# Attention and FFN interleaved on one core: score bursts of three chunks, PV one head at a time, FFN blocks partly in a score bank

## The chip, the cores and the metric

One NeuronCore of one Trainium2 chip. The metric is the device time of one execution in microseconds (us). The fast executions of the kernel before agree within about 1%. "Fast" and "slow" below are the states that each run lists; comparisons use fast runs. A ratio is the mean time of one kernel's fast runs over that of the other's of the same rounds, on the same chip, so it is not quite the ratio of the medians that are quoted.

Engines in the profile: PE is the matmul engine (TensorE), PEld its weight load, ACT is ScalarE (the exponentials), DVE is VectorE (copies, multiplies), POOL issues the loads, SPq is the queue of the transposing DMAs.

## The reference

```python
# q, k, v: (8, 8, 1152, 64); x: (4608, 512); dff = 1024
q_pool = q.reshape(B, H, S // 2, 2, D).mean(axis=3)      # 576 query rows a head
scores = matmul(q_pool, k.T) / sqrt(D)                   # softmax over 1152 keys
attn_out = softmax(scores) @ v                           # -> x, (B*576, 512)
a = x @ w1;  b = x @ w2
out = ((a * b) @ w3) @ w_out                             # T = w3 @ w_out is formed once
```

## The kernel before

Heads are worked in 32 pairs. A pair has 9 blocks of 128 keys times 576 queries; this stream of columns is cut in 324 chunks of 512. One chunk is a score tile of two PSUM banks (one a head), one exponential of 128x1024, and nine or so PV matmuls (exponentials times V) for both heads together, each with a 128x128 block of exponentials as weights. A burst is the score matmuls of the chunks of one iteration. FFN units of 512 tokens (96 matmuls of 512 columns, worked in blocks, each the matmuls into one bank) fill PE between them, as soon as their tokens are there. PE executes its matmuls in the order of the program.

The kernel uses eight PSUM banks: two score tiles (4), one accumulator for both heads (2), two FFN banks (2).

```python
def scores(c):                                   # one chunk, both heads (64-row tiles of PE)
    t = psum.tile([128, 2, CH], FP32, tag="psc", bufs=2, name="psc")
    ...
def attend(J, i):                                # PV: both heads, one after the other
    ...
        po[P] = psum.tile([128, 2, 512], FP32, tag="po", bufs=1, name="po")
    for u in range(2):
        nc.tensor.matmul(po[P][:, u, VW * i:VW * i + D + 1], er[:, u, r:r + 128],
                         vts[P % 4][:, u, j, 0:D + 1], ...)
def normalize(P):                                # DVE, once a pair: reciprocal, multiply
    ...
def bank(pre, wide):                             # FFN blocks: a bank of their own
    if not wide:
        return psum.tile([128, 512], FP32, tag="ff", bufs=2, name=pre)
...
for it in range(NIT):                            # 162 iterations of two chunks
    scores(2 * it);     expo(2 * it)
    scores(2 * it + 1); expo(2 * it + 1)
    ...
    for J, i in ready: attend(J, i)              # about 18 PV matmuls
    if last: normalize(...)
    fill(due)                                    # about five FFN matmuls
```

The softmax here doesn't subtract the row's maximum and nothing guards it: scores larger than these inputs give would overflow.

Of the kernel before, what the change touches and what calls it, by code (L numbers as in the profile page):

```python
# [18 lines left out]
RING = 4608  # L19
# [4 lines left out]
def kernel(  # L24
# [21 lines left out]
    T_AT = (8, 14)  # L46

    T_MM, T_TR, T_SC, T_AV = 0.216, 0.06, 0.63, 0.061
    PACE0, PACE1 = 2.2, 2.19
# [13 lines left out]
    w3T = const.tile([128, NF, NF, 128], FP16)  # L63
    wosb = const.tile([128, NF, dm], FP16)
# [86 lines left out]
    def prep_pe(P):  # L151
# [3 lines left out]
        t2 = psum.tile([128, 1024], FP16, tag="ff", bufs=2, name="t2")  # L155
        t1 = psum.tile([128, 1024], FP16, tag="ff", bufs=2, name="t1")
# [17 lines left out]
    def scores(c):  # L174
        t = psum.tile([128, 2, CH], FP32, tag="psc", bufs=2, name="psc")
# [20 lines left out]
    po = {}  # L196

    def attend(J, i):

        P, j = divmod(J, NJ)  # L200
        if j == 0 and i == 0:
            po[P] = psum.tile([128, 2, 512], FP32, tag="po", bufs=1, name="po")
        f = 128 * i if i < 4 else SQ - 128
        r = (J * SQ) % RING + f
        for u in range(2):
            nc.tensor.matmul(  # L206
                po[P][:, u, VW * i:VW * i + D + 1],
                er[:, u, r:r + 128],
                vts[P % 4][:, u, j, 0:D + 1],
                start=(j == 0 and i == 0), stop=(j == NJ - 1 and i == 4),  # L210
                skip_group_check=True)

    def normalize(P):
        acc = po.pop(P)[:, :, 0:5 * VW].rearrange("p u (i w) -> p u i w", w=VW)
        rz = ab.tile([128, 2, 5, 1], FP32, tag="rz", bufs=2, name="rz")
        nc.vector.reciprocal(out=rz, in_=acc[:, :, :, D:D + 1])  # L216
        xn = ab.tile([128, 5, 2, D], FP16, tag="xn", bufs=3, name="xn")
        nc.vector.tensor_tensor(  # L218
            out=xn.rearrange("p i u d -> p u i d"), in0=acc[:, :, :, 0:D],
            in1=rz.to_broadcast([128, 2, 5, D]), op=ALU.mult)  # L220
# [21 lines left out]
    def bank(pre, wide):  # L242
        if not wide:
            return psum.tile([128, 512], FP32, tag="ff", bufs=2, name=pre)
        return psum.tile([128, 2, 512], FP32, tag="psc", bufs=2, name=pre)[:, 0, :]

    def w3_transpose(c):
        t = psum.tile([128, 1024], FP16, tag="ff", bufs=2, name="w3t")
        for a in range(NF):
            nc.tensor.transpose(t[:, 128 * a:128 * a + 128],  # L250
                                w3h[c // 4][:, c % 4, 128 * a:128 * a + 128], ident)
        nc.vector.tensor_copy(out=w3T[:, c].rearrange("p a f -> p (a f)"), in_=t)

    def gen_T(half):

        cs = range(4 * half, 4 * half + 4)
        w3_transpose(cs[0])
        yield 8 * T_TR, True
        for c in cs:
            if c + 1 in cs:  # L260
                w3_transpose(c + 1)
                yield 8 * T_TR, True
            pt = bank("pT", False)
            for a in range(NF):
                nc.tensor.matmul(pt, w3T[:, c, a, :], wosb[:, a, :],  # L265
                                 start=(a == 0), stop=(a == NF - 1))
                if a < NF - 1:
                    yield T_MM, False
            nc.vector.tensor_copy(out=T16[:, c, :], in_=pt)  # L269
            yield T_MM, True  # L270

    def gen_ffn(t, tail):
        t0 = 512 * t
        gT = ffp.tile([128, NF, 512], FP16, tag="g", name="gT")
        for ft in range(NF):
            pa = bank("pa", tail and ft % 2)
            for mc in range(NC):
                nc.tensor.matmul(pa, w1sb[:, mc, ft * 128:ft * 128 + 128],  # L278
                                 xT[:, mc, t0:t0 + 512],
                                 start=(mc == 0), stop=(mc == NC - 1))  # L280
                if mc < NC - 1:
                    yield T_MM, False
            asb = ffp.tile([128, 512], FP32, tag="asb", name="asb")
            if tail:
                nc.scalar.copy(out=asb, in_=pa)  # L285
            else:
                nc.vector.tensor_copy(out=asb, in_=pa)  # L287
            yield T_MM, True
            pb = bank("pb", tail and ft % 2)
            for mc in range(NC):  # L290
                nc.tensor.matmul(pb, w2sb[:, mc, ft * 128:ft * 128 + 128],  # L291
                                 xT[:, mc, t0:t0 + 512],
                                 start=(mc == 0), stop=(mc == NC - 1))
                if mc < NC - 1:
                    yield T_MM, False
            nc.vector.tensor_mul(out=gT[:, ft, :], in0=pb, in1=asb)  # L296
            yield T_MM, True
        for i in range(4):
            pp = bank("pp", tail and i % 2)
            for ft in range(NF):  # L300
                nc.tensor.matmul(pp, gT[:, ft, 128 * i:128 * i + 128], T16[:, ft, :],  # L301
                                 start=(ft == 0), stop=(ft == NF - 1))
                if ft < NF - 1:
                    yield T_MM, False
# [54 lines left out]
    for it in range(NIT):  # L359
# [40 lines left out]
        if last:  # L400
            ready = ready[:last[0] + 1]
# [47 lines left out]
```

## Time and profile before

| | before |
|---|---|
| time | 449.42 us median of the first 3 runs (448.94 to 453.55) |
| PE / ACT / DVE busy | 93% / 73% / 44% |
| chain that ended last | 83% PE |
| one iteration (two chunks) in the middle | 2.26 us on average (most 2.0 to 2.5), 1.13 us a chunk |
| exponentials back to back | 0.92 us a chunk |

From the page of the kernel before: busy time of the engines, and the first line of the chain that ended last.

```profile
PE 419.4 (93%) x5168; PEld 223.1 (50%) x5168; DVE 198.2 (44%) x347; ACT 329.8 (73%) x350; POOL 70.0 (16%) x107
PE 83%; DMA 5%; ACT 4%; DVE 4%; issue 3%; SPq 1%; POOL 0%; ACTq 0%; DVEq 0%; POOLq 0%
```

PE bounds it. What PE waited for stands in the waits of engine PE: who waited for whom, then us in total, times, longest.

```profile
PE t_126 L158 <- DVE qp L119: 6.1, 1, 6.1
PE psc L187 <- DMA qT<-qp: 5.3, 1, 5.3
PE psc L187 <- ACT er L193: 4.2, 10, 0.7
PE po L206 <- DVE xn L218: 0.2, 1, 0.2
```

The 6.1 us are the start. The 5.3 us are one stall at 110 us. Waits of PV for the accumulator (`po`) are 0.2 us, and FFN lines do not wait for ACT at all.

One iteration in the timeline of the kernel before (start us, duration us, engine, line, output<-input, count; idle time before it in brackets):

```profile
231.44 0.61 PE L187 MATMUL psc<-qT,kT 64*128 64x512 f16 x6
231.93 1.94 ACT L193 ACTIVATE er<-psc 128x1024 f16<-128x1024 f32 x2 [0.49 <-PE psc L187]
231.98 0.72 PE L206 MATMUL po<-vt_78,er 128*128 128x65 f16 x18
232.54 1.02 PE L291 MATMUL pb<-xT,w2sb 128*128 128x512 f16 x4
233.40 0.38 PE L278 MATMUL pa<-xT,w1sb 128*128 128x512 f16 x1
233.71 0.39 PE L187 MATMUL psc<-qT,kT 64*128 64x128 f16 x4
```

Read PE by starts, because durations of matmuls overlap (a 512-column matmul is listed with 0.38 us and the next starts 0.215 us later). The burst takes 0.54 us, 18 PV 0.56, four FFN matmuls 0.86; the single `pa` takes 0.31 to the next score, 0.1 more than to another FFN matmul. ACT starts 0.49 us after the burst's first matmul.

The start-to-start times agree with the Trainium skill ("TensorE: Matmul & The Clock Gate", Back-to-back issue gap), which gives N/2.4 + 2.5 ns for a warm PE: it says 216 ns for 512 columns, and the trace has 215; worked out for 65 columns it gives an estimate of 29.6, and the trace has 29 to 30.

### The profile page before, as it was taken

The numbers are of one execution on the slowest core, as the hardware profiler recorded it, in microseconds if no ns is written. First come the engines' busy times: TensorE is split into PE (matmuls) and PEld (weight loads), VectorE is DVE, ScalarE is ACT, GpSimd is POOL, SyncE is SP. The second block draws the span as 40 slices with busy tenths as digits, with TensorE's granted clock in tenths as the row PEclk, the third lists the DMA queues.
The fourth block names the chain that finished last, engine by engine and source line by source line (L and its number), as shares of the span: only waits on it lengthen the run. The fifth ranks groups of instructions, "written<-read, shape, count | busy, mean of one in ns | idle before, by whom it ended". The sixth has DMA issues, their size and how long they took to land.

```text
span 448.8 us, 12036 instructions
## 1 busy us (share of the span) xinstructions
PE 419.4 (93%) x5168; PEld 223.1 (50%) x5168; DVE 198.2 (44%) x347; ACT 329.8 (73%) x350; POOL 70.0 (16%) x107
## 2 busy tenths in 40 slices
PE   2889898998699999999999999999999999989995
PEld 1555454554355555555555555545555555544442
DVE  2255454565235544554345444544554444433130
ACT  2977776777388888888888888888888888823332
POOL 7312130113011111111111111111100000000000
PEclk9999999999699999999999999999999999999999
DMA  8999999659999899999999999969882460131304
GB/s 137 209 188 206 208 190 182 94 94 126 154 182 150 129 111 204 167 144 126 148 179 130 134 173 183 132 117 164 167 155 57 92 106 18 15 70 39 89 6 93
DMA packets 94468, 59.11 MB, mean 132 GB/s; under 512 B 66256, under 2 KB 83664, under 8 KB 94416
## 3 DMA queue, kind: packets, MB, share of 16 engines
q0 software_dynamic: 25168, 33.56, 48.5%
q1 hardware_dynamic: 69248, 24.79, 35.1%
q8 instruction: 40, 0.66, 0.6%
q14 instruction: 12, 0.10, 0.1%
HBM read 67.11 MB, written 9.44 MB: 171 GB/s over the span
## 4 chain that ended last, share of the span: by engine, by line
PE 83%; DMA 5%; ACT 4%; DVE 4%; issue 3%; SPq 1%; POOL 0%; ACTq 0%; DVEq 0%; POOLq 0%
PE po L206 20%; PE psc L187 20%; PE pb L291 13%; PE pa L278 13%; PE pp L301 12%; ACT er L193 4%; PE pT L265 3%; DMA qT<-qp 3%; DMA vst<-in_v_dram 1%; DVE xn L218 1%; DVE kT L168 1%; PE w3t L250 1%; DMA out_dram<-osb 1%; DVE T_73 L269 0%; DVE osb L310 0%
## 5 line engine op out<-in xcount | busy, mean ns | idle before, releaser
L193 ACT ACTIVATE er<-psc 128x1024 f16<-128x1024 f32 x324 | 313.4, 1022 | 72.6 <-PE psc L187 69.8
L187 PE MATMUL psc<-qT,kT 64*128 64x512 f16 (+7 forms) x1152 | 109.2, 290 | 11.8 <-DMA qT<-qp 5.3
L206 PEld LDWEIGHTS <-er 128*128 128x128 f16 x2880 | 97.5, 98 | 35.5 <-issue 32.0
L187 PEld LDWEIGHTS <-kT 64*128 64x128 f16 x1152 | 44.4, 95 | 96.0 <-issue 84.5
L291 PE MATMUL pb<-xT,w2sb 128*128 128x512 f16 x288 | 79.7, 379 | 2.4 <-DVE osb L310 1.3
L278 PE MATMUL pa<-xT,w1sb 128*128 128x512 f16 x288 | 79.1, 379 | 1.2 <-DVE asb L287 0.7
L296 DVE TENSOR_TENSOR gT<-pb,asb 128x512 f16<-128x512 f32 x72 | 49.6, 688 | 64.1 <-PE pb L291 63.6
L301 PE MATMUL pp<-T_73,gT 128*128 128x512 f16 x288 | 71.4, 384 | 0.0
L287 DVE COPY asb<-pa 128x512 f32<-128x512 f32 x56 | 38.5, 688 | 47.1 <-PE pa L278 47.1
L90 POOL DMA_DIRECT2D kst<-in_k_dram x32 | 23.0, 718 | 221.3 <-DVE kc L135 175.1
L310 DVE TENSOR_SCALAR osb<-pp 128x512 f32<-128x512 f32 x28 | 19.3, 690 | 53.8 <-PE pp L301 51.4
L301 PEld LDWEIGHTS <-gT 128*128 128x128 f16 x288 | 25.7, 99 | 24.7 <-issue 1.1
L278 PEld LDWEIGHTS <-w1sb 128*128 128x128 f16 x288 | 25.8, 97 | 23.8 <-issue 0.7
L291 PEld LDWEIGHTS <-w2sb 128*128 128x128 f16 x288 | 25.4, 97 | 23.6 <-issue 1.6
L206 PE MATMUL po<-vt_80,er 128*128 128x65 f16 x720 | 29.6, 196 | 0.3 <-DVE xn L218 0.2
L206 PE MATMUL po<-vt_77,er 128*128 128x65 f16 x720 | 29.7, 195 | 0.0
L206 PE MATMUL po<-vt_78,er 128*128 128x65 f16 x720 | 28.7, 193 | 0.0
L206 PE MATMUL po<-vt_79,er 128*128 128x65 f16 x720 | 28.7, 193 | 0.0
L285 ACT COPY asb<-pa 128x512 f32<-128x512 f32 x16 | 9.4, 585 | 24.5 <-PE pa L278 24.5
L218 DVE TENSOR_TENSOR xn<-po,rz 128x640 f16<-128x640 f32 x32 | 26.4, 824 | 1.3 <-DVE rz L216 0.2
L97 POOL DMA_DIRECT2D vst<-in_v_dram x32 | 23.4, 732 | 16.6 <-DMA w3h<-in_moe_w_dram 10.3
L216 DVE RECIPROCAL rz<-po 128x10 f32<-128x10 f32 x32 | 7.1, 220 | 38.3 <-PE po L206 38.2
(80 smaller groups left out, 147.8 us busy)
## 6 DMA issues: line engine op xcount, KB each, us to landing
qst<-in_q_dram POOLq DMA_DIRECT2D x32, 288.0 KB, 7.1
kst<-in_k_dram POOLq DMA_DIRECT2D x32, 288.0 KB, 5.2
vst<-in_v_dram POOLq DMA_DIRECT2D x32, 288.0 KB, 9.0
out_dram<-osb SPq DMA_DIRECT2D x72, 128.0 KB, 3.3
w3h<-in_moe_w_dram POOLq DMA_DIRECT2D x2, 1024.0 KB, 20.5
wosb<-in_moe_w_out_dram POOLq DMA_DIRECT2D x1, 1024.0 KB, 19.5
xT<-xn SPq DMA_TRANSPOSE x64, 3.6
w1sb<-in_moe_w_dram POOLq DMA_DIRECT2D x1, 1024.0 KB, 22.0
```

The costliest lines, as they stand in the source:

```text
L90: nc.gpsimd.dma_start(out=kst[P].rearrange("p u j d -> p u (j d)"), in_=k[b, h0:h0 + 2].rearrange("u (p j) d -> p u (j d)", j=NJ))
L97: nc.gpsimd.dma_start(out=vst[P].rearrange("p u j d -> p u (j d)"), in_=v[b, h0:h0 + 2].rearrange("u (p j) d -> p u (j d)", j=NJ))
L187: nc.tensor.matmul(t[:, u, o:o + ln], kT[P][s, j, :], qv[s, f0:f0 + ln], start=True, stop=True)
L193: nc.scalar.activation(out=er[:, :, r:r + CH], in_=psc.pop(c), func=AF.Exp, bias=0.0, scale=SCALE)
L206: nc.tensor.matmul(po[P][:, u, VW * i:VW * i + D + 1], er[:, u, r:r + 128], vts[P % 4][:, u, j, 0:D + 1], start=(j == 0 and i == 0), stop= ...
L218: nc.vector.tensor_tensor(out=xn.rearrange("p i u d -> p u i d"), in0=acc[:, :, :, 0:D], in1=rz.to_broadcast([128, 2, 5, D]), op=ALU.mult)
L278: nc.tensor.matmul(pa, w1sb[:, mc, ft * 128:ft * 128 + 128], xT[:, mc, t0:t0 + 512], start=(mc == 0), stop=(mc == NC - 1))
L287: nc.vector.tensor_copy(out=asb, in_=pa)
L291: nc.tensor.matmul(pb, w2sb[:, mc, ft * 128:ft * 128 + 128], xT[:, mc, t0:t0 + 512], start=(mc == 0), stop=(mc == NC - 1))
L296: nc.vector.tensor_mul(out=gT[:, ft, :], in0=pb, in1=asb)
L301: nc.tensor.matmul(pp, gT[:, ft, 128 * i:128 * i + 128], T16[:, ft, :], start=(ft == 0), stop=(ft == NF - 1))
L310: nc.vector.tensor_scalar_mul(out=osb, in0=pp, scalar1=1.0 / (SCL * SCL))
```

## The change

The intent: fewer, longer score bursts, so that PE changes less often between score matmuls (half the rows a head) and the others, and a third score tile so that bursts do not wait for exponentials. The banks for it (6) come from two places: PV works one head at a time, so the accumulator is one bank, and FFN has only one bank of its own; every other FFN block goes into a score tile "in turn". The core of the diff:

```diff
-RING = 4608
+RING = 9216                                     # PV now runs about eight chunks behind
+    BURST = 3
-        t = psum.tile([128, 2, CH], FP32, tag="psc", bufs=2, name="psc")
+        t = psum.tile([128, 2, CH], FP32, tag="psc", bufs=3, name="psc")
...
-            po[P] = psum.tile([128, 2, 512], FP32, tag="po", bufs=1, name="po")
+            po[P, u] = psum.tile([128, 512], FP32, tag="po", bufs=1, name="po")
...                                              # normalize(P, u): once a head
+        if kind == "F":
+            return psum.tile([128, w], dt, tag="ff", bufs=1, name=pre)
+        return psum.tile([128, 2, w], dt, tag="psc", bufs=3, name=pre)[:, 0, :]
...                                              # x @ w1: kind X; x @ w2: kind F
+        for w in range(BURST):
+            scores(BURST * it + w)
+            expo(BURST * it + w)
...
-        lead = 0.5 if prepped < NPE else min(1.6, 0.5 + 0.5 * (prepped - NPE + 1))
+        if prepped < NP and at >= prepped - (0.65 if prepped < NPE else 1.75):
...
+        if peek() == "F":                       # a block left from the iteration before
+            run()
...                                              # parts: PV up to a change of heads, and after
+        head = 12 if len(parts[0]) > 12 else len(parts[0])
+        pv(parts[0][:head])
+        if x_free and peek() == "X" and done < quota:
+            run()
+        pv(parts[0][head:])
+        if peek() == "F" and done < quota:
+            run(quota)
+        pv(parts[1])
```

The output rows of the seven units inside the loop are made in halves of 256 columns. T = w3 @ w_out is formed at once and not in two halves. The count of score, PV and FFN columns stays the same. K and Q of the first eight pairs are still transposed by PE, now into a score tile; those of the later pairs are transposed by DMA, and their lead (how many pairs ahead they are prepared) is now 1.75 from the first such pair on.

More of the change, by code (lines that the diff above doesn't have):

```diff
@@ L45 @@
     NPE = 8
-    T_AT = (8, 14)
-    T_MM, T_TR, T_SC, T_AV = 0.216, 0.06, 0.63, 0.061
-    PACE0, PACE1 = 2.2, 2.19
+    BURST = 3
     SCALE = 0.5 * float(D) ** -0.5
@@ L62 @@
     T16 = const.tile([128, NF, dm], FP16)
-    w3T = const.tile([128, NF, NF, 128], FP16)
-    wosb = const.tile([128, NF, dm], FP16)
+    wosb = xT[:, :, NT - 1024:NT].rearrange("p m (h f) -> p m h f", h=2)
     er = const.tile([128, 2, RING], FP16)
@@ L154, in prep_pe @@
         kc = kcs.pop(P)
-        t2 = psum.tile([128, 1024], FP16, tag="ff", bufs=2, name="t2")
-        t1 = psum.tile([128, 1024], FP16, tag="ff", bufs=2, name="t1")
+        t12 = psum.tile([128, 2, 1024], FP16, tag="psc", bufs=3, name="t12")
+        t1, t2 = t12[:, 0, :], t12[:, 1, :]
         for c in range(NJ):
@@ L194, in expo, with attend, ready, normalize @@
                              bias=0.0, scale=SCALE)
-    po = {}
-    def attend(J, i):
-        P, j = divmod(J, NJ)
-        if j == 0 and i == 0:
-            po[P] = psum.tile([128, 2, 512], FP32, tag="po", bufs=1, name="po")
-        f = 128 * i if i < 4 else SQ - 128
-        r = (J * SQ) % RING + f
-        for u in range(2):
-            nc.tensor.matmul(
-                po[P][:, u, VW * i:VW * i + D + 1],
-                er[:, u, r:r + 128],
-                vts[P % 4][:, u, j, 0:D + 1],
-                start=(j == 0 and i == 0), stop=(j == NJ - 1 and i == 4),
-                skip_group_check=True)
-    def normalize(P):
-        acc = po.pop(P)[:, :, 0:5 * VW].rearrange("p u (i w) -> p u i w", w=VW)
-        rz = ab.tile([128, 2, 5, 1], FP32, tag="rz", bufs=2, name="rz")
-        nc.vector.reciprocal(out=rz, in_=acc[:, :, :, D:D + 1])
-        xn = ab.tile([128, 5, 2, D], FP16, tag="xn", bufs=3, name="xn")
-        nc.vector.tensor_tensor(
-            out=xn.rearrange("p i u d -> p u i d"), in0=acc[:, :, :, 0:D],
-            in1=rz.to_broadcast([128, 2, 5, D]), op=ALU.mult)
+    po, xns = {}, {}
+    def attend(n):
+        P, m = divmod(n, 90)
+        u, m = divmod(m, 45)
+        j, i = divmod(m, 5)
+        if m == 0:
+            po[P, u] = psum.tile([128, 512], FP32, tag="po", bufs=1, name="po")
+        f = 128 * i if i < 4 else SQ - 128
+        r = ((P * NJ + j) * SQ) % RING + f
+        nc.tensor.matmul(
+            po[P, u][:, VW * i:VW * i + D + 1], er[:, u, r:r + 128],
+            vts[P % 4][:, u, j, 0:D + 1],
+            start=(m == 0), stop=(m == 44), skip_group_check=True)
+    def ready(n, chunks):
+        P, m = divmod(n, 90)
+        j, i = divmod(m % 45, 5)
+        return (P * NJ + j) * SQ + min(128 * i + 128, SQ) <= chunks * CH
+    def normalize(P, u):
+        acc = po.pop((P, u))[:, 0:5 * VW].rearrange("p (i w) -> p i w", w=VW)
+        rz = ab.tile([128, 5, 1], FP32, tag="rz", bufs=2, name="rz")
+        nc.vector.reciprocal(out=rz, in_=acc[:, :, D:D + 1])
+        if u == 0:
+            xns[P] = ab.tile([128, 5, 2, D], FP16, tag="xn", bufs=3, name="xn")
+        xn = xns[P]
+        nc.vector.tensor_tensor(
+            out=xn[:, :, u, :], in0=acc[:, :, 0:D],
+            in1=rz.to_broadcast([128, 5, D]), op=ALU.mult)
+        if u == 0:
+            return
+        del xns[P]
         b, hp = divmod(P, 4)
@@ L240, in load_w @@
         nc.gpsimd.dma_start(out=dst, in_=src.rearrange("(c p) f -> p c f", p=128))
-    def bank(pre, wide):
-        if not wide:
-            return psum.tile([128, 512], FP32, tag="ff", bufs=2, name=pre)
-        return psum.tile([128, 2, 512], FP32, tag="psc", bufs=2, name=pre)[:, 0, :]
-    def w3_transpose(c):
-        t = psum.tile([128, 1024], FP16, tag="ff", bufs=2, name="w3t")
-        for a in range(NF):
-            nc.tensor.transpose(t[:, 128 * a:128 * a + 128],
-                                w3h[c // 4][:, c % 4, 128 * a:128 * a + 128], ident)
-        nc.vector.tensor_copy(out=w3T[:, c].rearrange("p a f -> p (a f)"), in_=t)
@@ L254, in gen_T @@
-    def gen_T(half):
-        cs = range(4 * half, 4 * half + 4)
-        w3_transpose(cs[0])
-        yield 8 * T_TR, True
-        for c in cs:
-            if c + 1 in cs:
-                w3_transpose(c + 1)
-                yield 8 * T_TR, True
-            pt = bank("pT", False)
-            for a in range(NF):
-                nc.tensor.matmul(pt, w3T[:, c, a, :], wosb[:, a, :],
-                                 start=(a == 0), stop=(a == NF - 1))
-                if a < NF - 1:
-                    yield T_MM, False
-            nc.vector.tensor_copy(out=T16[:, c, :], in_=pt)
-            yield T_MM, True
@@ L272, in gen_ffn, with load_wo, bank @@
-    def gen_ffn(t, tail):
+    def load_wo():
+        src = moe_w_out.rearrange("(m h p) f -> h p m f", p=128, h=2)
+        for h in range(2):
+            nc.gpsimd.dma_start(out=wosb[:, :, h, :], in_=src[h])
+    tail = False
+    turn = 0
+    def bank(pre, kind, dt=FP32):
+        nonlocal turn
+        w = 512 if dt == FP32 else 1024
+        if tail:
+            turn += 1
+            kind = "F" if turn % 4 == 0 else "X"
+        if kind == "F":
+            return psum.tile([128, w], dt, tag="ff", bufs=1, name=pre)
+        return psum.tile([128, 2, w], dt, tag="psc", bufs=3, name=pre)[:, 0, :]
@@ new lines, with T_groups, transposes, begin @@
+    w3T = {}
+    def T_groups():
+        def transposes(c):
+            def begin():
+                return bank("w3t", "X", FP16)
+            def mm(t, a):
+                nc.tensor.transpose(t[:, 128 * a:128 * a + 128],
+                                    w3h[c // 4][:, c % 4, 128 * a:128 * a + 128], ident)
+            def end(t):
+                w3T[c] = ab.tile([128, NF, 128], FP16, tag="w3T", bufs=3, name="w3T")
+                nc.vector.tensor_copy(out=w3T[c].rearrange("p a f -> p (a f)"), in_=t)
+            return "X", 0.25, NF, begin, mm, end
+        def products(c):
+            def begin():
+                return bank("pT", "F")
+            def mm(t, a):
+                nc.tensor.matmul(t, w3T[c][:, a, :], wosb[:, a // 2, a % 2, :],
+                                 start=(a == 0), stop=(a == NF - 1))
+            def end(t):
+                nc.vector.tensor_copy(out=T16[:, c, :], in_=t)
+            return "F", 1.0, NF, begin, mm, end
+        yield transposes(0)
+        for c in range(NF):
+            if c + 1 < NF:
+                yield transposes(c + 1)
+            yield products(c)
@@ L273, in gen_ffn, with ffn_groups, half, begin @@
+    def ffn_groups(t):
         t0 = 512 * t
         gT = ffp.tile([128, NF, 512], FP16, tag="g", name="gT")
-        for ft in range(NF):
-            pa = bank("pa", tail and ft % 2)
-            for mc in range(NC):
-                nc.tensor.matmul(pa, w1sb[:, mc, ft * 128:ft * 128 + 128],
+        asb = {}
+        def half(ft, w, kind):
+            def begin():
+                return bank("pa" if kind == "X" else "pb", kind)
+            def mm(p, mc):
+                nc.tensor.matmul(p, w[:, mc, ft * 128:ft * 128 + 128],
@@ L279, in gen_ffn, with end @@
                                  xT[:, mc, t0:t0 + 512],
                                  start=(mc == 0), stop=(mc == NC - 1))
-                if mc < NC - 1:
-                    yield T_MM, False
-            asb = ffp.tile([128, 512], FP32, tag="asb", name="asb")
+            def end(p):
+                if kind == "X":
+                    asb[ft] = ffp.tile([128, 512], FP32, tag="asb", name="asb")
+                    if tail:
+                        nc.scalar.copy(out=asb[ft], in_=p)
+                    else:
+                        nc.vector.tensor_copy(out=asb[ft], in_=p)
+                else:
+                    nc.vector.tensor_mul(out=gT[:, ft, :], in0=p, in1=asb.pop(ft))
@@ new lines, in half, with rows, begin, mm @@
+            return kind, 1.0, NC, begin, mm, end
+        def rows(i, s, wide):
+            n = 512 if wide else 256
+            kind = "F" if s else "X"
+            def begin():
+                return bank("pp", kind)
+            def mm(p, ft):
+                nc.tensor.matmul(p[:, 0:n], gT[:, ft, 128 * i:128 * i + 128],
+                                 T16[:, ft, n * s:n * s + n],
+                                 start=(ft == 0), stop=(ft == NF - 1))
+            def end(p):
+                if s == 0:
+                    osbs[i] = ffp.tile([128, dm], FP32, tag="osb", bufs=3, name="osb")
+                osb = osbs[i]
+                if tail:
+                    nc.scalar.activation(out=osb[:, n * s:n * s + n], in_=p[:, 0:n],
+                                         func=AF.Copy, bias=0.0, scale=1.0 / (SCL * SCL))
+                else:
+                    nc.vector.tensor_scalar_mul(out=osb[:, n * s:n * s + n], in0=p[:, 0:n],
+                                                scalar1=1.0 / (SCL * SCL))
+                if s == 1 or wide:
+                    for z in range(2):
+                        b, f = divmod(t0 + 128 * i + 64 * z, SQ)
+                        dst = out[b * SQ:(b + 1) * SQ, :].rearrange("(p c) m -> c p m", c=NJ)
+                        nc.sync.dma_start(out=dst[f // 64], in_=osb[64 * z:64 * z + 64, :])
+            return kind, (1.0 if wide else 0.5), NF, begin, mm, end
@@ L284, in gen_ffn @@
+        osbs = {}
+        for ft in range(NF):
+            yield half(ft, w1sb, "X")
+            yield half(ft, w2sb, "F")
+        for i in range(4):
             if tail:
-                nc.scalar.copy(out=asb, in_=pa)
+                yield rows(i, 0, True)
             else:
-                nc.vector.tensor_copy(out=asb, in_=pa)
-            yield T_MM, True
-            pb = bank("pb", tail and ft % 2)
-            for mc in range(NC):
-                nc.tensor.matmul(pb, w2sb[:, mc, ft * 128:ft * 128 + 128],
-                                 xT[:, mc, t0:t0 + 512],
-                                 start=(mc == 0), stop=(mc == NC - 1))
-                if mc < NC - 1:
-                    yield T_MM, False
@@ L296, in gen_ffn @@
-            nc.vector.tensor_mul(out=gT[:, ft, :], in0=pb, in1=asb)
-            yield T_MM, True
-        for i in range(4):
-            pp = bank("pp", tail and i % 2)
-            for ft in range(NF):
-                nc.tensor.matmul(pp, gT[:, ft, 128 * i:128 * i + 128], T16[:, ft, :],
-                                 start=(ft == 0), stop=(ft == NF - 1))
-                if ft < NF - 1:
-                    yield T_MM, False
-            osb = ffp.tile([128, dm], FP32, tag="osb", bufs=3, name="osb")
-            if tail:
-                nc.scalar.activation(out=osb, in_=pp, func=AF.Copy, bias=0.0,
-                                     scale=1.0 / (SCL * SCL))
-            else:
-                nc.vector.tensor_scalar_mul(out=osb, in0=pp, scalar1=1.0 / (SCL * SCL))
-            for s in range(2):
-                b, f = divmod(t0 + 128 * i + 64 * s, SQ)
-                rows = out[b * SQ:(b + 1) * SQ, :].rearrange("(p c) m -> c p m", c=NJ)
-                nc.sync.dma_start(out=rows[f // 64], in_=osb[64 * s:64 * s + 64, :])
-            yield T_MM, True
+                yield rows(i, 0, False)
@@ L319 @@
+                yield rows(i, 1, False)
     NCHUNK = NP * PAIR // CH
-    NIT = NCHUNK // 2
+    NIT = NCHUNK // BURST
+    NPV = NP * 90
     load_q(0)
@@ L331 @@
     load_w3(0)
-    load_w(wosb, moe_w_out)
+    load_wo()
     load(3)
@@ L341 @@
     n_units = NT // 512
-    filler = []
-    next_unit = 0
-    busy = due = 0.0
-    whole = True
-    blocks = [(J, i) for J in range(NP * NJ) for i in range(5)]
-    nb = 0
-    def fill(until, settle=False):
-        nonlocal busy, whole
-        while filler and (not whole if settle else busy < until):
-            try:
-                cost, whole = next(filler[0])
-                busy += cost
-            except StopIteration:
-                filler.pop(0)
+    EARLY = 7
+    RESERVE = 24.0
@@ new lines, with peek, run @@
+    gens = []
+    cur = None
+    place = None
+    step = 0
+    done = 0.0
+    def peek():
+        nonlocal cur, step
+        while cur is None and gens:
+            cur = next(gens[0], None)
+            step = 0
+            if cur is None:
+                gens.pop(0)
+        return cur and cur[0]
+    def run(until=None):
+        nonlocal cur, place, step, done
+        kind, cost, n, begin, mm, end = cur
+        while step < n and (until is None or done < until):
+            if step == 0:
+                place = begin()
+            mm(place, step)
+            step += 1
+            done += cost
+        if step == n:
+            end(place)
+            cur = None
@@ L359 @@
+    nb = 0
+    reached = []
+    next_unit = 0
+    quota = 0.0
+    t_left = True
     for it in range(NIT):
-        if it in T_AT:
-            filler.append(gen_T(T_AT.index(it)))
-        while next_unit < n_units:
+        at = it * BURST * CH / PAIR
+        if it == 5:
+            gens.append(T_groups())
+        while next_unit < EARLY:
             last_b = (512 * (next_unit + 1) - 1) // SQ
-            if (last_b + 1) * 4 * PAIR + 3 * 2 * CH > it * 2 * CH:
+            if it < 3 or reached[it - 2] < 360 * (last_b + 1):
@@ L366 @@
                 break
-            filler.append(gen_ffn(next_unit, False))
+            gens.append(ffn_groups(next_unit))
             next_unit += 1
-        scores(2 * it)
-        expo(2 * it)
-        scores(2 * it + 1)
-        expo(2 * it + 1)
-        busy += T_SC
-        due = (due if filler else busy - T_SC) + (PACE0 if it < 20 else PACE1)
-        at = it * 2 * CH / PAIR
-        if staged < NPE and at >= staged - 0.8:
+        for w in range(BURST):
+            scores(BURST * it + w)
+            expo(BURST * it + w)
@@ L377 @@
+        x_free = True
+        if staged < NPE and at >= staged - 1.0:
             prep_stage(staged)
             staged += 1
-            if waiting:
-                waiting.pop(0)()
+            for _ in range(2):
                 if waiting:
                     waiting.pop(0)()
-            else:
-                load(loaded)
-                loaded += 1
-        lead = 0.5 if prepped < NPE else min(1.6, 0.5 + 0.5 * (prepped - NPE + 1))
-        if prepped < NP and at >= prepped - lead:
-            if prepped < NPE:
-                fill(0, settle=True)
-                prep_pe(prepped)
-            else:
+                elif _ == 0:
+                    load(loaded)
+                    loaded += 1
@@ L392 @@
+        if prepped < NP and at >= prepped - (0.65 if prepped < NPE else 1.75):
+            if prepped >= NPE:
                 prep_dma(prepped)
@@ L394 @@
                 loaded += 1
-            prepped += 1
-        ready = [b for b in blocks[nb:nb + 40]
-                 if b[0] * SQ + min(128 * b[1] + 128, SQ) <= 2 * it * CH]
-        last = [n for n, (J, i) in enumerate(ready) if J % NJ == NJ - 1 and i == 4]
-        if last:
-            ready = ready[:last[0] + 1]
-        busy += T_AV * len(ready)
-        for J, i in ready:
-            attend(J, i)
-        if last:
-            normalize(ready[-1][0] // NJ)
-        nb += len(ready)
-        fill(due)
@@ L409 @@
-    for J, i in blocks[nb:]:
-        attend(J, i)
-    normalize(NP - 1)
-    for g in filler:
-        for _ in g:
-            pass
-    while next_unit < n_units:
-        for _ in gen_ffn(next_unit, True):
-            pass
-        next_unit += 1
+                prepped += 1
+            elif staged > prepped:
+                prep_pe(prepped)
+                prepped += 1
+                x_free = False
+        if gens or cur:
+            if next_unit == 0:
+                quota = done + 9.0
+            else:
+                left = 96.0 * EARLY + 80.0 - RESERVE - done
+                quota = done + left / (NIT - it)
@@ new lines, with pv @@
+        if peek() == "F":
+            run()
+        want = min(NPV, int(NPV / NCHUNK * BURST * (it + 1 - 2.7)))
+        parts = [[], []]
+        cut = None
+        while nb < want and ready(nb, BURST * it):
+            if cut is None and nb % 45 == 0 and (parts[0] or parts[1]):
+                cut = 1
+            parts[1 if cut else 0].append(nb)
+            nb += 1
+        reached.append(nb)
+        def pv(ns):
+            for n in ns:
+                attend(n)
+                if n % 45 == 44:
+                    normalize(n // 90, n // 45 % 2)
@@ new lines @@
+        head = 12 if len(parts[0]) > 12 else len(parts[0])
[6 more added lines that the diff above has]
+        pv(parts[1])
+    while nb < NPV:
+        attend(nb)
+        if nb % 45 == 44:
+            normalize(nb // 90, nb // 45 % 2)
+            if nb % 90 == 44:
+                if peek() == "F":
+                    run()
+                for _ in range(2):
+                    if peek():
+                        run()
+        nb += 1
@@ L422 @@
+    tail = True
+    while peek():
+        run()
+    for t in range(next_unit, n_units):
+        gens.append(ffn_groups(t))
+    while peek():
+        run()
 _INS = ['q', 'k', 'v', 'moe_w1', 'moe_w2', 'moe_w3', 'moe_w_out']
```

## The prediction

> **What bounds it now.** The page gives PE 93% busy, ACT 73%, DVE 44%; the chain of waits is 83% PE. In the timeline (140 to 400 us) an iteration of two chunks takes 2.2 to 2.3 us, 1.13 us a chunk: scores 0.54, 18 PV matmuls of 0.031, about five FFN matmuls of 0.216. ACT needs 0.92 us a chunk (start to start when not starved), so it is second: some bursts take 0.75 us because their second chunk waits for a score bank. Single losses: a 5.3 us stall for the DMA of qT at 110 us and a lower clock after it (about 8 us in all), and a start of 10 us.
>
> **What the change saves.** From an FFN matmul to a score matmul it is 311 ns start to start instead of 215, and a burst of 1024 columns a head takes 544 ns against about 430 of streaming: 0.2 us a burst beside its columns. The Trainium skill ("TensorEngine Tiling (Array Packing)", Key Properties) says that changing the tiling mode drains the TensorE; these 0.2 us agree. 162 bursts become 108: 11 us saved. The third score buffer removes about half of 17 us of second-chunk waits, and the longer DMA lead the 8 us stall. PV, FFN and tail work stay the same (256-column output halves add under 1 us).
>
> **What it adds: waits on PE.**
> 1. The first FFN block of an iteration takes the score bank that the first exponential frees. That exponential starts 0.494 us after the burst's first matmul, runs 1.022 us, and a waiting PE starts 0.051 us later: 1.57 us. PE arrives after the burst (0.77) and 12 PV (0.37) at 1.14 us, and stalls 0.42 us, except where work left over from a block fills it. About 75 iterations: 30 us.
> 2. The PV accumulator is one bank, handed over 64 times instead of 32. From the last PV matmul: 0.24 us to DVE's start, reciprocal 0.22, multiply about 0.49 (estimate from 0.82 for 640 columns), 0.05 back: 1.0 us, more when the copy of the X block (0.69 us) is ahead in DVE's queue. The FFN block put there lasts 0.86 us, or is missing: about 0.45 us each, 28 us.
> 3. K/Q transposes in PE now wait for an exponential: 7 times 0.8 us.
>
> A typical iteration becomes 1.57 + X 0.86 + 15 PV 0.47 + F 0.86 + entry 0.10 = 3.85 us for three chunks, 1.28 a chunk, although ACT would allow 2.76. An FFN unit (96 matmuls) comes only every 13.5 iterations, so seven iterations have none and run at 2.1 to 3 us.
>
> **Sum.** 449 - 11 - 8 - 8 - 8 (FFN-bank waits of the early phase) + 30 + 28 + 6 = 478 us. PE runs in order and is the bound, so its waits are on the critical path.
>
> **What would show it.** PE busy falls to about 85%; in the waits, PE idle for ACT at the pa/pp lines (20 to 35 us) and for DVE xn at the PV line (20 to 30 us), both nearly zero before; iterations near 3.9 us; ACT's share below 70%; no 5 us DMA stall. The tail after the last exponential stays near 50 us.
>
> **What would make it wrong.** If the normalising hides behind F, about 460. If X waits less than 0.2 us, even or faster. New DMA stalls in the early phase would add.
>
> Predicted 478 us, range 461 to 492; faster 0.07, same 0.09, slower 0.84.

## The result, and the profile after

The changed kernel took 481.42 us (479.8 to 484.11, 4 runs), the kernel before 450.59 in the same and earlier rounds: ratio 1.068, 95% interval 1.063 to 1.074.

The page of the changed kernel, the same two lines:

```profile
PE 418.6 (87%) x5376; PEld 259.4 (54%) x5376; DVE 209.6 (44%) x435; ACT 325.3 (68%) x352; POOL 70.3 (15%) x108
PE 63%; ACT 20%; DVE 7%; DMA 4%; issue 4%; POOL 0%; ACTq 0%; POOLq 0%
```

PE is busy for the same 419 us, in a span 31 us longer. Of the chain that ended last, PE lost 20 points, ACT gained 16 and DVE 3, although ACT's own share of busy time fell: the chain now goes through an exponential in most iterations. The waits of engine PE in the changed kernel:

```profile
PE po L203 <- DVE xn L220: 17.9, 27, 1.4
PE pa L312 <- ACT er L189: 13.6, 44, 0.6
PE t L154 <- DVE qp L115: 6.1, 1, 6.1
PE t L154 <- ACT er L189: 4.5, 7, 0.7
PE pp L335 <- ACT er L189: 3.4, 11, 0.6
PE psc L183 <- ACT er L189: 3.2, 9, 0.5
PE pa L312 <- DMA xT<-xn: 1.1, 1, 1.1
```

The first was 0.2 us before, the second, fourth and fifth are new, and the DMA wait for qT is gone. One iteration in the timeline of the changed kernel, with a change of heads at its end:

```profile
198.27 0.83 PE L183 MATMUL psc<-qT,kT 64*128 64x192 f16 x12
198.76 2.85 ACT L189 ACTIVATE er<-psc 128x1024 f16<-128x1024 f32 x3 [1.11 <-PE psc L183]
199.03 0.54 PE L203 MATMUL po<-vt,er 128*128 128x65 f16 x12
199.84 1.02 PE L312 MATMUL pa<-xT,w1sb 128*128 128x512 f16 x4 [0.27 <-ACT er L189]
200.70 0.59 PE L203 MATMUL po<-vt,er 128*128 128x65 f16 x14
200.90 0.69 DVE L322 COPY asb<-pa 128x512 f32<-128x512 f32 x1 [0.77 <-PE pa L312]
201.12 1.03 PE L312 MATMUL pb<-xT,w2sb 128*128 128x512 f16 x4
201.51 0.18 DVE L216 RECIPROCAL rz<-po 128x5 f32<-128x5 f32 x1
201.73 0.49 DVE L220 TENSOR_TENSOR xn<-po,rz 128x320 f16<-128x320 f32 x1
202.28 0.20 PE L203 MATMUL po<-vt,er 128*128 128x65 f16 x1
202.41 0.83 PE L183 MATMUL psc<-qT,kT 64*128 64x384 f16 x10
```

- The 12 PV matmuls need 0.37 us, so PE could start `pa` at 199.40. It starts at 199.84: its bank is that of the burst's first exponential, which runs from 198.76 for 1.03 us. The 14 PV matmuls behind it have their data and wait too. This is the first stall, 0.44 us; the profile lists only 0.27, because it counts the modelled tail of the last PV matmul as busy.
- The last of the 14 PV matmuls closes a head at about 201.1. DVE is still copying `pa`, so the reciprocal begins at 201.51; the multiply ends at 202.22; PV goes on at 202.28. The four `pb` matmuls end, by starts, at 201.98. This is the second stall, 0.3 us here.
- The iteration takes 4.14 us for three chunks, of which ACT works 2.85.

Why must `pa` wait at all? Its bank, `[:, 0, :]` of a score tile, holds the first head's scores, which that exponential is still reading: `pa` would overwrite them. Nor would another part of the bank do. The Trainium skill ("PSUM — Partial Sum Buffer", PSUM bank collisions raise a hardware error) asks for a guard by bank between an engine that writes and one that still reads, and the kernel has that guard. No run here shows a collision; the traces show the price of the wait, PE starting 51 ns after the exponential's end when it waits. The same skill ("PSUM — Partial Sum Buffer", Engine vs sequencer instructions) says that matmuls start and complete in program order, and the trace agrees: the 14 PV matmuls do not overtake.

PE's time by starts shows where the 31 us are. For each matmul the time to the next matmul's start is taken; beyond the normal gap (31 ns for PV, 215.5 for 512 columns, 109 for 256) it is a wait of the next one, or, up to 0.15 us before a score, an entry into a burst. The division into rows is by these rules, so a row is good to some tenths of a us.

| us, from the traces | before | after | difference |
|---|---|---|---|
| score bursts (first score to first other matmul) | 107.9 | 95.7 | -12.2 |
| of it the stall for the DMA of qT | 5.6 | 0 | -5.6 |
| of it K/Q transposes waiting for an exponential (beyond 0.2 us each) | 0 | 5.6 | +5.6 |
| entries into bursts | 15.0 | 10.1 | -4.9 |
| PV and FFN matmuls, transposes, without waits | 301.4 | 301.7 | +0.3 |
| waits of the first FFN block, `pa`, `pp`, `w3t` | 3.5 | 33.2 | +29.7 |
| waits of PV for the accumulator | 0.3 | 23.9 | +23.6 |
| other waits | 9.7 | 4.6 | -5.1 |
| sum over all matmul starts | 437.8 | 469.3 | +31.5 |

A burst of two chunks takes 544 ns (median) before, one of three takes 759 after. The 33.2 us are 77 stalls of 0.41 us on average (31.9 us), and a small rest. The 23.9 us are not spread over all changes of heads: 33 of 63 wait 0.2 us or more, 0.72 us on average, and the other 30, with more work of other kinds in the gap, do not wait.

### The profile page after: what moved, and what is told of

Its sections match the earlier page's. It is cut to its first block, busy times and chain, and to the rows that moved or that the text cites. A ratio compares the mean times of both kernels' runs of the same rounds, so it can differ in the third digit from the quotient of the medians.

```text
span 480.3 us, 12530 instructions
## 1 busy us (share of the span) xinstructions
PE 418.6 (87%) x5376; PEld 259.4 (54%) x5376; DVE 209.6 (44%) x435; ACT 325.3 (68%) x352; POOL 70.3 (15%) x108
## 4 chain that ended last, share of the span: by engine, by line
PE 63%; ACT 20%; DVE 7%; DMA 4%; issue 4%; POOL 0%; ACTq 0%; POOLq 0%
ACT er L189 19%; PE pa L312 15%; PE pp L335 12%; PE po L203 12%; PE pb L312 10%; PE psc L183 9%; DVE xn L220 3%; PE pT L289 2%; DMA qT<-qp 2%; DVE asb L322 1%; DMA xT<-xn 1%; DMA vst<-in_v_dram 1%; PE t L159 1%; PE w3t L276 1%; DVE rz L216 1%
## 5 line engine op out<-in xcount | busy, mean ns | idle before, releaser
L203 PEld LDWEIGHTS <-er 128*128 128x128 f16 x2880 | 111.3, 98 | 61.9 <-DVE xn L220 30.2
L203 PE MATMUL po<-vt,er 128*128 128x65 f16 x2880 | 127.0, 194 | 18.5 <-DVE xn L220 17.9
L183 PE MATMUL psc<-qT,kT 64*128 64x512 f16 (+7 forms) x1152 | 94.3, 290 | 5.3 <-ACT er L189 3.2
L335 PE MATMUL pp<-T,gT 128*128 128x256 f16 (+1 forms) x496 | 73.8, 290 | 3.5 <-ACT er L189 3.4
L183 PEld LDWEIGHTS <-kT 64*128 64x128 f16 x1152 | 44.2, 95 | 41.8 <-issue 20.5
L335 PEld LDWEIGHTS <-gT 128*128 128x128 f16 x496 | 45.2, 98 | 22.9 <-issue 9.7
L347 DVE TENSOR_SCALAR osb<-pp 128x256 f32<-128x256 f32 x52 | 22.1, 425 | 56.9 <-PE pp L335 56.7
L220 DVE TENSOR_TENSOR xn<-po,rz 128x320 f16<-128x320 f32 x64 | 31.5, 492 | 2.2
L79 POOL DMA_DIRECT2D qst<-in_q_dram x32 | 19.5, 610 | 14.1 <-DMA w2sb<-in_moe_w_dram 5.6
L216 DVE RECIPROCAL rz<-po 128x5 f32<-128x5 f32 x64 | 12.1, 188 | 20.5 <-PE po L203 20.5
L124 DVE COPY vt<-vst 128x1152 f16<-128x1152 f16 x32 | 17.0, 530 | 1.1 <-DMA vst<-in_v_dram 1.1
```

The source lines that it names most:

```text
L79: nc.gpsimd.dma_start(out=qst[P // 2][o:o + 64].rearrange("p u t d -> p u (t d)"), in_=q[b, h0:h0 + 2].rearrange("u (p t) d -> p u (t d)", ...
L183: nc.tensor.matmul(t[:, u, o:o + ln], kT[P][s, j, :], qv[s, f0:f0 + ln], start=True, stop=True)
L203: nc.tensor.matmul(po[P, u][:, VW * i:VW * i + D + 1], er[:, u, r:r + 128], vts[P % 4][:, u, j, 0:D + 1], start=(m == 0), stop=(m == 44), ...
L220: nc.vector.tensor_tensor(out=xn[:, :, u, :], in0=acc[:, :, 0:D], in1=rz.to_broadcast([128, 5, D]), op=ALU.mult)
L335: nc.tensor.matmul(p[:, 0:n], gT[:, ft, 128 * i:128 * i + 128], T16[:, ft, n * s:n * s + n], start=(ft == 0), stop=(ft == NF - 1))
L347: nc.vector.tensor_scalar_mul(out=osb[:, n * s:n * s + n], in0=p[:, 0:n], scalar1=1.0 / (SCL * SCL))
```

## The experiments

Nine kernels were run, all with correct results. Medians below are of fast runs. The numbers of the expectations were added up from durations in the traces along each kernel's order of instructions. The theory: the new waits, `pa` for the exponential and PV for the accumulator, are on the critical path and cost about 30 and 24 us. The main rival: they are slack, since PE would wait for the same exponentials at the next burst anyway, and the finer PV work (one head at a time, 64 normalisings instead of 32) is what costs.

### x_late: the first FFN block behind all PV of the first part

```diff
-        head = 12 if len(parts[0]) > 12 else len(parts[0])
+        head = len(parts[0])
```

> The first FFN block of an iteration moves behind all PV matmuls of the first part (up to the change of heads) instead of behind 12 of them; nothing else changes. Theory (PE stalls for the first exponential, about 32 us measured start to start in the trace of after, and for the accumulator, about 24 us): PE now arrives after 0.77 + up to 27 x 0.031 us, mostly later than 1.57 us, and where a head change falls late in the iteration both FFN blocks stand in its gap, so more than half of both stalls goes: 450 us, 443 to 458; PE idle for ACT at the pa and pp lines falls from 17 us to under 9. Rival (the stall is slack: without it PE waits for the same exponentials at the next burst, or the single-head PV work itself is what costs): 475 to 482 us.

Measured: 455.1 us (three fast runs, 452.2 to 457.6), ratio to the kernel before 1.011 (1.005 to 1.017). One line took back some 26 of the 31 us, with the same buffers, bursts and PV order. The theory holds and the rival falls. The profile of this run fell in the slow state (460.5 us, clock 0.992), so its time is not read, and the sizes of its waits only roughly. Waits of engine PE in x_late:

```profile
PE po L203 <- DVE xn L220: 8.9, 9, 1.4
PE pa L312 <- DMA xT<-xn: 6.0, 5, 2.7
PE pa L312 <- ACT er L189: 4.8, 11, 0.6
```

Both stalls fell by about half or more. A new one stands beside them: FFN is now so early that it waits for the transpose of its tokens by DMA, 6.0 us, which was 1.1 us in the changed kernel. That may be part of why it missed the 450 us in the middle of the expected range; no fast run was profiled to show it.

### x_soon: the same block straight behind the burst

```diff
-        head = 12 if len(parts[0]) > 12 else len(parts[0])
+        head = 0
```

> The opposite dose: the first FFN block stands straight behind the score burst, before any PV matmul. Theory: each iteration with such a block stalls about 0.37 us (12 PV) more, about 77 to 85 iterations: 481 + 31 = 512 us, 505 to 520; PE idle for ACT at pa and pp rises from 17 us to about 45. Rival (slack): within 5 us of 481.

Measured: 521.6 us (520.7 to 524.0), ratio 1.160. The direction and the lines are as expected; the size is 40 us and not 31, just outside the range. Waits of engine PE in x_soon:

```profile
PE pa L312 <- ACT er L189: 36.6, 56, 0.7
PE po L203 <- DVE xn L220: 23.7, 40, 1.4
PE pp L335 <- ACT er L189: 9.5, 20, 0.7
```

The block waits 46.1 us in the profile, as expected (45). The excess is in the second line: the accumulator waits rose too, from 17.9 to 23.7 us (from 23.9 to 33.6 by starts). By the program's order, where the change of heads fell within the first 12 PV matmuls, both FFN blocks stood in its gap in the changed kernel, and here only the second does.

### norm2: the normalising multiply done twice

```diff
             out=xn[:, :, u, :], in0=acc[:, :, 0:D],
             in1=rz.to_broadcast([128, 5, D]), op=ALU.mult)
+        nc.vector.tensor_tensor(
+            out=xn[:, :, u, :], in0=acc[:, :, 0:D],
+            in1=rz.to_broadcast([128, 5, D]), op=ALU.mult)
```

> The changed kernel with the multiply of the normalising done twice (same values, 64 more DVE operations of 0.49 us, DVE is 44% busy). Theory (PE waits for the accumulator bank at nearly every change of heads that has at most one FFN block in it): 64 x 0.49 = 31 us more DVE work, of which about 20 us show: 501 us, 494 to 510; PE idle for DVE xn at the PV line rises from 18 us to about 36. Rival (handover hidden, DVE is not a bound): within 4 us of 481.

Measured: 502.2 us (501.1 to 503.1), 20.8 us over the changed kernel, as expected. PE's wait for the accumulator:

```profile
PE po L203 <- DVE xn L223: 37.5, 40, 1.9
```

It was 17.9 us in 27 waits. DVE, 48% busy in this run, costs time because PE stands behind one of its chains, not because it is full. By starts the accumulator waits went from 23.9 to 44.3 us, the whole difference, and the waits for the exponential stayed (33.2 and 32.8).

### mid8: another order of the same blocks

```diff
-        if peek() == "F":
-            run()
...
-        head = 12 if len(parts[0]) > 12 else len(parts[0])
+        head = len(parts[0]) if cut else 8
         pv(parts[0][:head])
+        if peek() == "F":
+            run()
         if x_free and peek() == "X" and done < quota:
             run()
         pv(parts[0][head:])
-        if peek() == "F" and done < quota:
-            run(quota)
         pv(parts[1])
```

The F block, whose bank is free, comes first and gives the exponential its time; both blocks stand at the change of heads.

> The same blocks in another order in each iteration: burst, 8 PV matmuls (or all of the head's rest where the head changes), then the second FFN block left from the iteration before (its own bank, waits for nothing), then the first FFN block of the next pair, then the rest of PV. Theory: the first block arrives at 0.77 + 0.25 + 0.86 = 1.88 us, after the 1.57 us that the exponential needs, and a change of heads has 1.72 us of FFN in it against 1.0 us of handover: about 45 us of stalls go: 436 us, 430 to 444, faster than the kernel before by 2 to 4%. Rival (bursts of three or single-head PV are slower in themselves): not below 450 us.

Measured: 443.1 us (440.7 to 445.3; a fourth run was slow, 452.1), ratio to the kernel before 0.985 (0.979 to 0.990): 38 us below the changed kernel and below the kernel before. The median lies in the range, but "2 to 4% faster" was too much: it is 1.5%, which at a threshold of 2% counts as unclear. The page and the waits of engine PE in mid8:

```profile
PE 407.7 (92%) x5376; PEld 261.9 (59%) x5376; DVE 213.1 (48%) x435; ACT 325.0 (74%) x352; POOL 70.5 (16%) x108
PE po L203 <- DVE xn L220: 4.5, 6, 1.4
PE pa L312 <- DMA xT<-xn: 1.4, 1, 1.4
PE pa L312 <- ACT er L189: 1.3, 4, 0.4
```

By starts the waits of the first block are 7.5 us (33.2 in the changed kernel) and those for the accumulator 5.7 (23.9), so 44 us went, about the 45 expected. The score bursts grew from 95.7 to 102.1 us: some 6 us of it come back as waits inside bursts, 2.1 of them for the copy of an output row by DVE. To that extent, at most, the rival was right.

### mid8_split: the burst cut once

```diff
         for w in range(BURST):
+            if w == 2:
+                pv(parts[0][:4])
             scores(BURST * it + w)
             expo(BURST * it + w)
...
-        head = len(parts[0]) if cut else 8
-        pv(parts[0][:head])
+        head = max(4, len(parts[0]) if cut else 8)
+        pv(parts[0][4:head])
```

> The kernel of the run mid8 with four PV matmuls moved from behind the burst to between its second and third chunk, so each iteration changes twice more between score and PV matmuls; number of matmuls, buffers and FFN order as in mid8. If a burst costs 0.2 us beside its columns, as the prediction took it, 108 more bursts cost up to 21 us, less what hides in iterations that wait for ACT: mid8 plus 11 to 20 us, 455 to 464. If the time of a burst lies in its columns and chunks alone (no saving from longer bursts): mid8 within 3 us.

Measured: 463.4 us (461.5 to 464.5), 20.2 us over mid8. Entries into bursts rose from 10.0 us (105) to 20.5 us (210) by starts, 0.1 us each; the burst and PV times rose by 3.6 and 3.4 us. Nearly all of the 3.4 us goes with a lower clock and not with the number of bursts: the granted clock was 0.988 here and 1.000 in the profile of mid8, and the FFN and PV matmuls that follow each other at about twice the usual distance add up to 3.3 us here and 0.2 there. So longer bursts do pay, 0.13 us (entries and bursts alone) to 0.19 us (all of the 20.2) for each one saved, somewhat under the 0.2 of the prediction: the change's idea was sound.

### before_lead: the longer DMA lead in the kernel before

```diff
-        lead = 0.5 if prepped < NPE else min(1.6, 0.5 + 0.5 * (prepped - NPE + 1))
+        lead = 0.5 if prepped < NPE else 1.75
```

> The kernel before with one thing of the change: K and Q that are transposed by DMA are prepared 1.75 pairs ahead from the first such pair on, not 1.0 growing to 1.6. Prediction's term: the 5.3 us stall of the score matmul for the DMA of qT at 110 us and the lower clock after it go, about 8 us: 442 us, 439 to 445, and no PE wait for that DMA over 1 us. Rival (the stall comes from the DMA queues being full of loads then, whatever the lead): 447 to 452 with the stall at another place.

Measured: 451.6 us, ratio 1.002 (0.999 to 1.004). The expected 439 to 445 us was missed, and nothing gained; the wait of PE stands where it was:

```profile
PE psc L187 <- DMA qT<-qp: 6.0, 1, 6.0
```

The transfer of that qT took 17.2 us from issue to landing (the longest of the run), 12.5 in the kernel before. It was a weak test: the preparation of the pair before still gates this one, so it was issued only 2.6 us earlier (100.4 against 103.0 us), and the landing came no earlier. In this kernel the lead alone does not help.

### after_lead: the shorter lead in the changed kernel

```diff
-        ... (0.65 if prepped < NPE else 1.75):
+        ... (0.65 if prepped < NPE else min(1.6, 0.5 + 0.5 * (prepped - NPE + 1))):
```

> The changed kernel with the lead of the kernel before (1.0 pair for the first pair transposed by DMA, growing to 1.6). In the trace of after, K of that pair is copied at 99.1 us, its qT transfer is issued at 103.5 us and takes up to 11 us, and the first score matmul on it runs at 115.4 us, so it is just in time. If the longer lead is what took the 8 us stall away: preparation one iteration (4 us) later brings a PE wait of 2 to 5 us for the DMA of qT back, 483 to 487 us. If the slower pace of the changed kernel took it away: no such wait over 1 us and 481 within 3 us.

Measured: 487.6 us (486.1 to 489.3), 6.1 us over the changed kernel and just above the expected 483 to 487. The DMA waits of PE:

```profile
PE pa L312 <- DMA xT<-xn: 3.2, 3, 1.7
PE psc L183 <- DMA qT<-qp: 1.7, 1, 1.7
```

The wait for qT came back, with 1.7 us smaller than expected, and the one for the tokens grew from 1.1 to 3.2. So in the changed kernel the lead matters; in the kernel before it did not suffice. The two of them together fit a transfer that lands just in time at the slower pace; what fills the DMA queues at that point was not taken apart.

### mid8_kq and kq65: K/Q transposes behind the free FFN block

```diff
             elif staged > prepped:
-                prep_pe(prepped)
-                prepped += 1
                 x_free = False
...                                              # behind the F block of mid8:
-        if x_free and peek() == "X" and done < quota:
+        if not x_free:
+            prep_pe(prepped)
+            prepped += 1
+        elif peek() == "X" and done < quota:
             run()
```

mid8_kq also stages them 0.75 instead of 0.65 pairs ahead; kq65 does not.

> The kernel of mid8, and the K and Q transposes on PE (7 times, first 95 us) stand behind the FFN block that waits for nothing, in place of the first FFN block, and are staged 0.75 instead of 0.65 pairs ahead. In mid8 PE waits 4.1 us for ACT at their first line. Theory: those 0.6 us a time go, and part of the queueing of head changes behind their copies on DVE: 4 us less than mid8, 440 us, 434 to 444, over 1.5% faster than the kernel before. Rival (the early phase is bound by ACT or loads): as mid8, 444.

> The kernel of mid8_kq with the staging of its PE transposes back at 0.65 pairs. The fast runs of mid8_kq took 437 to 441 us, and two of six were slow (454 and 461), the profiled one with PE waits of 7.0 us for an output row and 5.6 us for qT behind full DMA queues near 110 to 145 us. Theory: same saving over mid8 in the fast runs (438 to 443 us); whether the DMA waits show is a matter of when loads and transposes meet, so some runs may again be 10 to 20 us longer. Rival (0.75 caused the pile-up): all six within 3 us of each other.

Measured: mid8_kq 438.2 us in four fast runs (436.8 to 441.0), ratio to the kernel before 0.973 (0.970 to 0.976); two of its six runs were slow (454.1 and 461.3). kq65: 440.8 us in six fast runs (439.7 to 446.1), ratio 0.977 (0.976 to 0.979); one of seven was slow (448.7). Both beat both kernels, by 2.3 to 2.7% over the kernel before. In kq65 the transposes' wait for ACT, 4.5 us in the changed kernel and 4.1 in mid8, is 0.3 us. Its profiled run was the slowest of the fast ones (446.1 us), and PE waits in it for the transposes of FFN tokens, 1.4 us in mid8:

```profile
PE pa L312 <- DMA xT<-xn: 5.7, 3, 4.0
PE t L154 <- ACT er L189: 0.3, 1, 0.3
```

The one profile of mid8_kq fell in the slow state (clock 0.977). It shows what PE waited for in that run, and not why the runs differ:

```profile
PE psc L183 <- DVE osb L347: 7.0, 1, 7.0
PE psc L183 <- DMA qT<-qp: 5.6, 2, 3.0
```

There a qT transfer took up to 24.1 us to land (11.0 in the changed kernel's profile), and PE stood 7.0 us behind a score bank whose output row could not be copied out yet, because the copy waited for a store. The 7.0 us wait falls where six stores of output rows stood in the DMA queue. As kq65 also had one slow run and one at 446, the staging alone is not the cause; which transfers meet was left open.

## Why the prediction was right

The prediction of 478 us was 3.4 us below the median of 481.42, inside 461 to 492. That the number came so close is in part luck: the savings were taken 7 us too large (35 against 27.7) and the costs 5 us too large (64 against 58.9), and the two errors cancel for the most part. Its terms against the accounting by starts:

| term | predicted | measured |
|---|---|---|
| fewer bursts, and third score buffer | -11 and -8 | -17 (bursts without the two special waits -12.2, entries -4.9); the two not separated |
| the qT stall and the lower clock | -8 | -5.6 for the stall; after it the bursts, PV and FFN matmuls of 116 to 122 us took some 2.4 us longer than usual in the kernel before (lower clock), which the accounting keeps in other rows |
| other early waits on FFN banks | -8 | -5.1 |
| first FFN block waits for an exponential | +30 | +29.7 |
| accumulator handed over 64 times | +28 | +23.6 |
| K/Q transposes wait for an exponential | +6 | +5.6 |

- The step that decided it was the cycle time of an iteration: score, 0.49 us to the exponential, 1.02 us, 0.05 us to PE, then X, 15 PV, F and the entry, 3.85 us. The trace has many iterations of 3.84 and 3.85 us, and most of those with a change of heads take 3.8 to 4.5. The term of 75 stalls of 0.42 us is right in both factors (77 of 0.41). x_late and x_soon moved only that block, mid8 both FFN blocks, and the time followed.
- The handover of the accumulator was right in mechanism (norm2) and 4 us too large. Its factors were not right: about 0.45 us at each of 64 changes was predicted, and 0.72 us at 33 of 63 was measured; that the product fits is luck.
- "The longer DMA lead removes the 8 us stall" was only half right. The stall went, but before_lead shows that the lead alone does not remove it in the kernel before; after_lead shows that it counts in the changed one.
- Of the marks to look for: PE busy 87% (said about 85), ACT 68% (below 70), iterations near 3.9 us, the tail 54 us after the last exponential (53 before; said near 50). PE idle for ACT at `pa` and `pp` is 17.0 us and for `xn` 17.9, both under the ranges of 20 to 35 and 20 to 30: the prediction mixed up times by starts with the idle times of that view, which leave out about 0.16 us a wait.

## What to carry to other kernels

When blocks of work share PSUM banks in rotation, follow one iteration by times: a block that takes the bank of the first reader of this very burst makes a cycle out of two engines that ran side by side, and PE's order then holds back everything behind it. Put work that waits for nothing between, and put enough of it where an accumulator changes hands; here the order of the same blocks was worth 38 us, more than the longer bursts saved. A wait is worth only as much as comes behind it, so test it by moving the waiting block both ways and not by busy shares.

## What the Trainium skill lacked or had wrong

- "TensorEngine Tiling (Array Packing)", Key Properties, says that a change of tiling mode drains the TensorE and gives no time. Here an entry into score matmuls, where the mode changes, cost 96 ns (311 against 215 start to start), a burst took about 117 ns beyond its columns (544 against 427 for 1024 columns a head, 759 against 640 for 1536, at 2.4 columns a ns), and each further burst 0.13 to 0.19 us in all (mid8_split). No run separates the drain from whatever else an entry costs.
- "TensorE: Matmul & The Clock Gate", Back-to-back issue gap, gives sustained spacings for pairs of weight load and matmul of about 81 ns at 128 columns and 131 ns at 512. Every matmul here loads its own weights, and the spacing was 29 to 30 ns at 65 columns, 55 to 56 at 128 (the transposes of w3) and 215 at 512: the formula that the page calls isolated holds, and the sustained figures do not.
- No page was found that gives the whole way of a bank from PE to ACT and back: here 0.49 us from the first score matmul of a chunk to the start of its exponential, and 51 ns from the end of that to a matmul that waited for it.
